# Convolution taps all on VectorE, and two of the small sums made by ScalarE and an adding DMA, in a convolution and hard-swish layer on one Trainium2 core

## The chip, the cores and the metric

The kernel runs on one core of a Trainium2 chip. The metric is device time in microseconds (us) of one launch. TensorE (PE) multiplies matrices, VectorE (DVE), ScalarE (ACT) and GpSimd (POOL) work on tiles, and SyncE (SP) issues transfers. Each of them takes its instructions in the order in which they were written down. Transfers (DMAs) are issued by SP, by POOL and by ACT and are carried by 16 DMA engines that all issuers share. A DMA issued by POOL can add what it carries to what already stands at its destination; this kernel uses that in place of additions on an engine.

## The reference

```python
# x: (8, 4096, 192), weight: (8, 7), w_in: (192, 2048), w_out: (2048, 192), all float32 in use
w = softmax(weight, axis=-1)                    # 8 heads x 7 taps
x_pad = concat([zeros(8, 6, 192), x], axis=1)   # causal
conv[b, s, head] = sum_k w[head, k] * x_pad[b, s + k, head]   # 24 channels per head
h = conv.reshape(32768, 192) @ w_in             # first layer
g = h * clip(h + 3, 0, 6) / 6
out = g @ w_out                                 # second layer
```

The two weight matrices arrive as 64-bit floats and are rounded in the kernel; x arrives transposed, channels ahead of time.

## The kernel before

The 32,768 tokens are worked in 32 blocks of 1,024, each as two groups of 512 that lie on the two halves of the partitions. Block 0 is computed in a plain way while the weights are prepared. Blocks 1 to 31 run the loop `for i in range(1, NB)` at the end of the kernel: `first_layer(i, jobs)` and then `second_layer(i, between)`.

**Convolution.** `y` (128 x 1536) holds the convolution of the next block. It takes seven steps, made by `conv_jobs`: ACT writes `x * c0` (L1030), and six taps add `x shifted by k, times c_k` to it. A tap is one DVE instruction (L1032). One of the six goes another way, `tap_by_dma` (L1019): POOL multiplies x into `S3` (L1021) and then issues a DMA that adds `S3` to `y` (L1025). When `y` is finished it is split into three parts, HIGH (ACT, L476), LOW (DVE, `split_low`, L1055) and MIX (DVE, `split_mix`, L479), from which the first layer gets float32 precision out of fast matmuls. Three pairs of POOL DMAs copy the parts to the other half of the partitions (`y_other`, L266 and L267).

**First layer.** 16 units, `n` = 0 to 15; units 0 to 7 read `y_own`, 8 to 15 `y_other`. A unit is 12 matmuls (`begin`), a multiplication in PSUM by ACT (L523), 6 more matmuls (`end`), then `relu` on ACT (L302) and `gate` on DVE (L306), which writes `g`. Four pairs of PSUM banks go round, so `begin(n + 4)` needs the banks that `gate(n)` gives back. In the last unit the multiplication is shared: ACT takes the lower bank (L526), DVE the upper (L527). `jobs[n]` is what is recorded behind unit n, `jobs[-1]` ahead of unit 0: here the convolution's taps, and `left`, the two `finish` steps that end the block before. On POOL, small sums of `g` into `shared` follow units 1, 3, 5 and 7, and then sums of `A22`, differences `S3` and DMAs that make `S1` (L561).

**Second layer.** `g` is read as a 2 x 2 matrix of quarters A11, A21, A12, A22, and the product is made in Strassen's way with seven products, some of them split a second time into seven small ones. For the first level the sums are S1 = A21 + A22, S2 = S1 - A11, S3 = A11 - A21, S4 = A12 - S2; S4 is written over S3, pair of chunks by pair of chunks, by `negative`: ACT writes -S2 (L696) and a POOL DMA adds A12 to it (L697). For the second level `small_sums(to, x, which, ...)` (L573) makes four sums of the quarters of x; `A12`'s go to `sums2` (a part of the tile `z2`), `S1`'s to `s5`, which is A22's place in `g`, and `A22`'s to `sums4`. The fourth sum is the second quarter of x less the second sum.

The order is written out by hand. PE's matmuls stand in four streams of 80 ticks each that run side by side in four column groups, and `do(t, fn)` records other engines' work at tick `t - 0.5`. All is sorted by tick and recorded in that order, so each engine's own order follows from the ticks. PE has one queue: when a matmul of one stream waits, the matmuls recorded behind it, of all four streams, wait as well. What the change touches stands at these ticks: product 7 with S3 up to tick 44; the small product (2, 3), which reads the fourth sum of A12, at ticks 60 to 64; product 3, which reads the four pairs of S4, from ticks 64, 68, 72 and 76; the small product (5, 3), which reads the fourth sum of S1, at ticks 72 to 76. `between` has the work for the next blocks: the taps left over at tick 24, `begin_conv` (a load of x by SP, into the one buffer that the taps have read) at 30, the split of y at 37, 62 and 63, its copies to the other half at 70, and the first step of the next convolution at 74.

Of the kernel before, what the change touches and what calls it, by code (L numbers as in the profile page):

```python
# [8 lines left out]
ALU = mybir.AluOpType  # L9
# [16 lines left out]
def kernel(  # L26
# [8 lines left out]
    nc = tc.nc  # L35
# [3 lines left out]
    H, KC = weight.shape  # L39
# [3 lines left out]
    N = 512  # L43
# [3 lines left out]
    K3 = D // D2  # L47
# [29 lines left out]
    def load_x(i, dma=nc.sync):  # L77
        x = xs.tile([P, K3, PAD + N], F32, name="x")
        head, lower, upper = x_source(i)
        if head:  # L80
            nc.vector.memset(x[0:D2, :, 0:PAD], 0.0)
        dma.dma_start(out=x[0:D2, :, head:], in_=lower)
        dma.dma_start(out=x[D2:P, :, :], in_=upper)
        return x
# [3 lines left out]
    for base, dma in ((0, nc.scalar), (D2, nc.sync)):  # L88
        dma.dma_start(
            out=w_sb[base : base + D2],  # L90
            in_=weight.unsqueeze(1).to_broadcast([H, GJ, KC]),
# [126 lines left out]
    for n in range(AHEAD):  # L218
# [8 lines left out]
        out=e_sb[:], in0=w_sb[:], in1=mx[:].to_broadcast([P, KC]), op=ALU.subtract  # L227
# [3 lines left out]
    c_sb = cst.tile([P, KC], F32, name="c_sb")  # L231
# [5 lines left out]
    y = ys.tile([P, K3, N], F32, name="y")  # L237
# [36 lines left out]
    A11, A21, A12, A22 = (g4[:, :, j] for j in range(4))  # L274
    S2, S1, S4 = A11, A21, A12
# [181 lines left out]
    def add(out, x, y, op=ALU.add):  # L457
        nc.vector.tensor_tensor(out=out, in0=x, in1=y, op=op)
# [33 lines left out]
    def swap_parts(dma=nc.sync, parts=range(3)):  # L492
        if parts[0] == HIGH:
            y_other[0] = pools[1].tile([P, 3, K3, N], F32, name="y_other", tag="other")
        for n in parts:
            swap(y_other[0][:, n], y_own[n], dma)
# [73 lines left out]
    def four_parts(x):  # L570
        return [x[:, c::2, t] for t in halves for c in range(2)]
# [30 lines left out]
    def second_layer(i, between):  # L602
# [3 lines left out]
        z = pools[1].tile([P, NP + 1, N], F32, name="z2", tag="other")  # L606
        sums2, p1 = z[:, 0:NP], z[0:DH, NP]
        ends = [psum[:, 2 * free_slots[0] + k] for k in range(2)] if last else [b, b]
        s5 = A22
# [21 lines left out]
        def do(t, fn, *args, **kw):  # L631
            streams[3].append((t - 0.5, lambda: fn(*args, **kw)))  # L632
# [58 lines left out]
        def fold(p, m136):  # L691
            add(p[second, hi], p[second, hi], p[second, lo])
            add(p[second, lo], m136, p[second, lo])

        def negative(pair):
            nc.scalar.mul(S3[:, pair], S2[:, pair], -1.0)  # L696
            nc.gpsimd.dma_start(out=S3[:, pair], in_=A12[:, pair], accum_op=ALU.add)  # L697

        def after(j, fn, *args, **kw):
            do(clock[j], fn, *args, **kw)  # L700
# [36 lines left out]
        left = [list(every) for _ in halves]  # L737
# [72 lines left out]
        do(32, fold_with, p1)  # L810
        do(33, g_sums, nc.vector, (2,), every[4:], 4)
        do(35, copy, out=b[m], in_=p1)
        do(36, small_sums, s5, S1, (1, 2, 3, 4), nc.vector)
        do(37, small_sums, sums2, A12, (4,), nc.vector)
        do(38, fold_with, p4, 2)
        for n, t in zip(range(0, NP, 2), (34, 39, 42, 45)):
            do(t, negative, slice(n, n + 2))
# [85 lines left out]
    with tc.manual_schedule():  # L903
# [4 lines left out]
            out=c_sb[:], in0=e_sb[:], in1=sm[:].to_broadcast([P, KC]), op=ALU.mult  # L908
# [15 lines left out]
        for _ in range(3):  # L924

            nc.tensor.matmul(
                out=psum[:, b], lhsT=zeros[:, 0:P], rhs=zeros[:], start=True, stop=True
# [58 lines left out]
        n = 3  # L986
# [29 lines left out]
        late = ctx.enter_context(tc.tile_pool(name="late", bufs=1, reuse_waits="tile"))  # L1016
        w_in_parts = [late.tile([P, NP, K3, P], F32, name=f"w_in{n}") for n in range(3)]

        def tap_by_dma(x, k):  # L1019
            to = S3[:, 0:K3]  # L1020
            nc.gpsimd.tensor_scalar(  # L1021
                out=to, in0=x[:, :, k : k + N], scalar1=c_sb[:, k : k + 1], scalar2=None,
                op0=ALU.mult,
            )
            nc.gpsimd.dma_start(out=y[:], in_=to, accum_op=ALU.add)  # L1025

        def conv_jobs(i):
            x = x_tiles.pop(i)
            conv_x[:] = [x]
            jobs = [lambda: nc.scalar.mul(y[:], x[:, :, 0:N], c_sb[:, 0:1])]  # L1030
            for k in range(1, KC):
                jobs.append(lambda k=k: nc.vector.scalar_tensor_tensor(  # L1032
                    out=y[:], in0=x[:, :, k : k + N], scalar=c_sb[:, k : k + 1], in1=y[:],
                    op0=ALU.mult, op1=ALU.add,
                ))
            return jobs
# [24 lines left out]
        def prepare():  # L1061
            for n in range(0, NP, 4):
                r = slice(n, n + 4)
                w_parts(*[w[:, r] for w in w_in_parts], w_in[:, r])
            for job in conv_jobs(1):
                job()
            first_in.close()
            later = ctx.enter_context(tc.tile_pool(name="later", bufs=1, reuse_waits="tile"))
            pools.append(later)
            pools.append(ctx.enter_context(tc.tile_pool(name="oth", bufs=1, reuse_waits="tile")))  # L1070
            x_tiles[2] = load_x(2, nc.gpsimd)
            split_y()

        conv, conv_x = [], []

        def begin_block_two():
            w_sums(((T1, B12, B11), (T2, B22, T1), (T4, B21, T2)))
            small_weights([(w_s[:, n], w) for n, w in enumerate((B11, T1, B21, T4))])
            conv.extend(conv_jobs(2))
            for job in conv[:2]:  # L1080
                job()
# [5 lines left out]
        S3 = last.tile([P, NP, N], F32, name="s3")[:]  # L1087
        left = []
        taps = conv[2:]
        for i in range(1, NB):  # L1090
            jobs = {3 + 2 * n: [tap] for n, tap in enumerate(taps[:5]) if n}
            k = KC - len(taps)
            jobs[-1] = [lambda: tap_by_dma(conv_x[0], k)] * bool(taps) + left
            first_layer(i, jobs)
            now = taps[5:]

            def begin_conv():
                x_tiles[i + 2] = load_x(i + 2)
                conv[:] = conv_jobs(i + 2)

            between = [(24, tap) for tap in now]
            conv = []
            if i + 1 < NB:
                between += [(37, split_high), (62, split_low), (63, split_mix)]
                between += [
                    (t, lambda n=n: swap_parts(nc.gpsimd, (n,)))
                    for n, t in ((HIGH, 70), (LOW, 70), (MIX, 70))
                ]
            if i + 2 < NB:
                between += [(30, begin_conv), (74, lambda: conv[0]())]  # L1110
            left = second_layer(i, between)
            taps = conv[1:]

# [32 lines left out]
```

## Time and profile before

| what | us |
|---|---|
| median of 3 runs (2389.35 to 2394.75) | 2394.53 |
| the profiled execution, its device time | 2391.43 |
| its span, first to last instruction | 2389.6 |
| PE busy in the span | 2271.1 |
| DVE busy | 2019.1 |
| ACT busy | 1694.2 |
| POOL busy | 1364.8 |
| PE idle ahead of first-layer matmuls (L511) | 84.5 |
| PE idle ahead of second-layer matmuls (L635) on `g` | 21.9 |

The profile is of one execution; its times are 0.1% under the median of the runs. A group in the profile is a source line, an engine, an operation and its operands, with the number of its instructions, their busy time in us, the mean of one in ns, and the idle time of the engine just before them with what ended it. The trace behind it has the start and the end of each instruction. Lines of helpers such as L584 (`small_sums`) or L635 (`matmul`) gather the work of several callers, so groups are told apart by operands and shapes: the sums of `S1` on DVE are `g<-g 128x1024`, those of `A12` and `A22` `z<-...`.

### The profile page before, as it was taken

How to read it: one execution, taken by the hardware profiler on the slowest of the kernel's cores; microseconds unless marked ns; L12 is line 12 of the kernel's file. 1: busy time of each engine (PE TensorE's matmuls, PEld its weight loads, DVE VectorE, ACT ScalarE, POOL GpSimd, SP SyncE). 2: the span in 40 equal slices, each digit the busy share in tenths (PEclk: the TensorE clock that was granted, in tenths of full speed). 3: DMA queues.
4: the chain of work that ended last, by engine and by line, in shares of the span. 5: the costliest groups of instructions: out<-in, count | busy, mean ns of one | idle time of the engine just before them, and what ended most of it. 6: DMA issues, size and time to landing. Idle time of an engine off the chain costs nothing.

```text
span 2389.6 us, 55082 instructions
## 1 busy us (share of the span) xinstructions
PE 2271.1 (95%) x22984; PEld 1479.5 (62%) x22984; DVE 2019.1 (84%) x1891; ACT 1694.2 (71%) x2329; POOL 1364.8 (57%) x1155
## 2 busy tenths in 40 slices
PE   9999999999999999999999999999999999999998
PEld 5456666666665566665666656666556666566665
DVE  8788888888788988889888898888898888988876
ACT  7567776677776777766777667677667776677765
POOL 2556665556655566555666455665556655566644
PEclk9999999999999999999999999999999999999999
DMA  5356668666676656685666766667755677566665
GB/s 146 81 100 122 116 116 151 116 113 116 117 142 131 109 114 118 134 151 96 118 121 124 147 117 113 114 119 142 139 101 112 116 137 147 101 118 119 123 122 85
DMA packets 308521, 288.00 MB, mean 121 GB/s; under 512 B 211472, under 2 KB 216592, under 8 KB 308272
## 3 DMA queue, kind: packets, MB, share of 16 engines
q0 software_dynamic: 86560, 225.55, 49.9%
q1 hardware_dynamic: 220472, 58.67, 13.5%
q8 instruction: 180, 2.95, 0.5%
q14 instruction: 69, 0.57, 0.1%
q10 hardware_dynamic: 1240, 0.27, 0.1%
HBM read 31.72 MB, written 25.17 MB: 24 GB/s over the span
## 4 chain that ended last, share of the span: by engine, by line
PE 51%; DMA 16%; DVE 12%; POOL 10%; issue 7%; ACT 3%; SPq 1%; DVEq 0%; POOLq 0%; ACTq 0%
PE psum L635 41%; DMA y<-s 11%; PE psum L511 7%; DVE g L306 6%; DVE y L1032 5%; POOL s L1021 4%; DMA out_dram<-shared 3%; PE psum L296 2%; PE psum L341 2%; POOL y_other L267 2%; POOL y_other L266 1%; ACT psum L632 1%; POOL shared L584 1%; DMA g<-g 1%; ACT g L302 1%
## 5 line engine op out<-in xcount | busy, mean ns | idle before, releaser
L635 PE MATMUL psum<-g,w_out 128*32 128x512 f32 (+1 forms) x5968 | 904.3, 520 | 21.9 <-DMA g<-g 12.6
L306 DVE SCALAR_TENSOR_TENSOR g<-g,psum 128x1024 f32<-128x1024 f32 (+1 forms) x528 | 613.3, 1182 | 189.5 <-ACT g L302 189.4
L635 PE MATMUL psum<-s,w_out 128*32 128x512 f32 (+1 forms) x3024 | 676.0, 587 | 1.2 <-DMA s<-g 1.2
L511 PE MATMUL psum<-y_other,w_in 64*128 64x512 f32 x4464 | 552.2, 393 | 84.5 <-DVE psum L527 51.4
L302 ACT ACTIVATE g<-psum,half 128x1024 f32<-128x1024 f32 (+1 forms) x528 | 567.4, 1087 | 50.9 <-PE psum L511 50.0
L511 PEld LDWEIGHTS psum<-y_other,w_in 64*128 64x128 f32 x4464 | 422.7, 185 | 203.0 <-DVE psum L527 64.0
L523 ACT ACTIVATE psum<-psum 128x1024 f32<-128x1024 f32 x465 | 469.0, 1009 | 102.0 <-PE psum L511 100.0
L635 PEld LDWEIGHTS psum<-g,w_out 128*32 128x32 f32 x5968 | 355.3, 113 | 297.1 <-issue 126.5
L511 PE MATMUL psum<-y_own,w_in 64*128 64x512 f32 x4464 | 521.9, 388 | 0.0
L511 PEld LDWEIGHTS psum<-y_own,w_in 64*128 64x128 f32 x4464 | 424.2, 184 | 105.4 <-issue 26.0
L697 POOL DMA_DIRECT2D s<-g x124 | 148.4, 1197 | 431.8 <-ACT s L696 405.9
L1032 DVE SCALAR_TENSOR_TENSOR y<-x,c_sb,y 128x1536 f32<-128x1536 f32 x156 | 351.7, 2255 | 46.4 <-DMA y<-s 44.2
L584 POOL TENSOR_TENSOR shared<-g 128x256 f32<-128x256 f32 x248 | 230.3, 929 | 103.0 <-DVE g L306 103.0
L635 PE MATMUL psum<-g,w_s 128*32 128x256 f32 x1488 | 283.5, 380 | 0.0
L635 PEld LDWEIGHTS psum<-s,w_out 128*32 128x32 f32 x3024 | 187.8, 110 | 85.8 <-issue 24.9
L635 PE MATMUL psum<-z,w_out 128*32 128x256 f32 x992 | 235.1, 380 | 2.4
L635 PE MATMUL psum<-z,w_s 128*32 128x256 f32 x992 | 237.0, 383 | 0.3 <-DVE z L584 0.2
L584 POOL TENSOR_TENSOR z<-g 128x1024 f32<-128x1024 f32 x62 | 205.3, 3311 | 0.0
L266 POOL DMA_DIRECT2D y_other<-y_own x90 | 48.8, 542 | 265.3 <-issue 246.6
L561 POOL DMA_DIRECT2D g<-g x124 | 150.0, 1224 | 86.4 <-DVE s L414 61.9
L414 POOL TENSOR_TENSOR s<-g 128x1024 f32<-128x1024 f32 x62 | 163.6, 2639 | 0.0
L414 DVE TENSOR_TENSOR g<-g 128x2048 f32<-128x2048 f32 x62 | 142.0, 2290 | 19.9 <-issue 18.9
(115 smaller groups left out, 2973.3 us busy)
## 6 DMA issues: line engine op xcount, KB each, us to landing
y_other<-y_own POOLq DMA_DIRECT2D x180, 384.0 KB, 8.1
g<-g POOLq DMA_DIRECT2D x124, 512.0 KB, 5.5
s<-g POOLq DMA_DIRECT2D x124, 512.0 KB, 6.6
out_dram<-shared SPq DMA_DIRECT2D x378, 64.0 KB, 5.5
y<-s POOLq DMA_DIRECT2D x30, 768.0 KB, 11.0
x<-in_x_dram SPq DMA_DIRECT2D x53, 388.5 KB, 5.7
stage<-in_moe_w_in_dram SPq DMA_DIRECT2D x16, 192.0 KB, 5.1
stage<-in_moe_w_out_dram SPq DMA_DIRECT2D x8, 384.0 KB, 5.5
```

Of the source, the lines that this page charges most:

```text
L266: dma.dma_start(out=to[D2:P], in_=part[0:D2])
L302: nc.scalar.activation(r6, h, ACT.Relu, bias=half[:], scale=1.0 / 6.0)
L306: nc.vector.scalar_tensor_tensor(out=g_, in0=g_, scalar=1.0, in1=h, op0=ALU.min, op1=ALU.mult)
L414: engine.tensor_tensor(out=o[:, r], in0=a[:, r], in1=b[:, r], op=op)
L511: nc.tensor.matmul(out=psum[:, 2 * slots[n] + k], lhsT=r32(w_in_parts[part][r, c, s]), rhs=r32(y_other[0][r, part, s] if group else y_own[ ...
L523: nc.scalar.mul(both(n), both(n), 4097.0)
L561: nc.gpsimd.dma_start(out=S1[:, pair], in_=A22[:, pair], accum_op=ALU.add)
L584: engine.tensor_tensor(out=o, in0=p, in1=q, op=op)
L635: nc.tensor.matmul(out=out, lhsT=w, rhs=x, start=start, stop=True, tile_position=(0, j * QS), skip_group_check=True,)
L697: nc.gpsimd.dma_start(out=S3[:, pair], in_=A12[:, pair], accum_op=ALU.add)
L1021: nc.gpsimd.tensor_scalar(out=to, in0=x[:, :, k : k + N], scalar1=c_sb[:, k : k + 1], scalar2=None, op0=ALU.mult,)
L1032: jobs.append(lambda k=k: nc.vector.scalar_tensor_tensor(out=y[:], in0=x[:, :, k : k + N], scalar=c_sb[:, k : k + 1], in1=y[:], op0=ALU.mu ...
```

## The change

- `tap_by_dma` is gone. All six taps of a block are DVE instructions. Four are recorded in the first layer, ahead of unit 0 and behind units 1, 3 and 5; before, they stood behind units 5, 7, 9 and 11, and the tap by DMA ahead of unit 0. Two are recorded at tick 24 of the second layer, before it was one.
- `left` is recorded ahead of the tap that stands ahead of unit 0.
- The fourth small sum of A12 and that of S1 leave DVE. A new `last_sum` lets ACT write the negated second sum into the place of the fourth, and a POOL DMA adds the quarter of A12 or S1. They are recorded at ticks 29 and 50; before, DVE made them behind the other sums at 37 and 36.
- `split_low` moves from tick 62 to 56, `begin_conv` from 30 to 27.

```diff
+        def difference(out, x, y):
+            nc.scalar.mul(out, y, -1.0)
+            nc.gpsimd.dma_start(out=out, in_=x, accum_op=ALU.add)
+
         def negative(pair):
-            nc.scalar.mul(S3[:, pair], S2[:, pair], -1.0)
-            nc.gpsimd.dma_start(out=S3[:, pair], in_=A12[:, pair], accum_op=ALU.add)
+            difference(S3[:, pair], A12[:, pair], S2[:, pair])
+
+        def last_sum(to, x):
+            z = four_parts(to)
+            difference(z[3], four_parts(x)[1], z[1])
...
-        do(36, small_sums, s5, S1, (1, 2, 3, 4), nc.vector)
-        do(37, small_sums, sums2, A12, (4,), nc.vector)
+        do(29, last_sum, sums2, A12)
+        do(36, small_sums, s5, S1, (1, 2, 3), nc.vector)
+        do(50, last_sum, s5, S1)
...
-        def tap_by_dma(x, k):
-            to = S3[:, 0:K3]
-            nc.gpsimd.tensor_scalar(
-                out=to, in0=x[:, :, k : k + N], scalar1=c_sb[:, k : k + 1], scalar2=None,
-                op0=ALU.mult,
-            )
-            nc.gpsimd.dma_start(out=y[:], in_=to, accum_op=ALU.add)
-
...
-            jobs = {3 + 2 * n: [tap] for n, tap in enumerate(taps[:5]) if n}
-            k = KC - len(taps)
-            jobs[-1] = [lambda: tap_by_dma(conv_x[0], k)] * bool(taps) + left
+            jobs = {2 * n - 1: [tap] for n, tap in enumerate(taps[:4])}
+            jobs[-1] = left + jobs.get(-1, [])
             first_layer(i, jobs)
-            now = taps[5:]
+            now = taps[4:]
...
-                between += [(37, split_high), (62, split_low), (63, split_mix)]
+                between += [(37, split_high), (56, split_low), (63, split_mix)]
...
-                between += [(30, begin_conv), (74, lambda: conv[0]())]
+                between += [(27, begin_conv), (74, lambda: conv[0]())]
```

The fourth parts are 128 partitions x 4 chunks x 256 floats, so a row of the new transfers is 1 KB long; a row of those of `negative` is 2 KB, two rows to a partition. Each of them carries 512 KB.

More of the change, by code (lines that the diff above doesn't have):

```diff
@@ L1017 @@
         w_in_parts = [late.tile([P, NP, K3, P], F32, name=f"w_in{n}") for n in range(3)]
-        def tap_by_dma(x, k):
-            to = S3[:, 0:K3]
-            nc.gpsimd.tensor_scalar(
-                out=to, in0=x[:, :, k : k + N], scalar1=c_sb[:, k : k + 1], scalar2=None,
-                op0=ALU.mult,
-            )
-            nc.gpsimd.dma_start(out=y[:], in_=to, accum_op=ALU.add)
         def conv_jobs(i):
             x = x_tiles.pop(i)
-            conv_x[:] = [x]
             jobs = [lambda: nc.scalar.mul(y[:], x[:, :, 0:N], c_sb[:, 0:1])]
@@ L1072, in prepare @@
             split_y()
-        conv, conv_x = [], []
+        conv = []
         def begin_block_two():
```

## The prediction

> **What bounds the kernel now.** First the page: busy time by engine, then the groups.
>
> ```profile
> PE 2271.1 (95%) x22984; PEld 1479.5 (62%) x22984; DVE 2019.1 (84%) x1891; ACT 1694.2 (71%) x2329; POOL 1364.8 (57%) x1155
> ...
> L1032 DVE SCALAR_TENSOR_TENSOR y<-x,c_sb,y 128x1536 f32<-128x1536 f32 x156 | 351.7, 2255 | 46.4 <-DMA y<-s 44.2
> L584 DVE TENSOR_TENSOR g<-g 128x1024 f32<-128x1024 f32 x124 | 146.1, 1220 | 1.1
> ...
> L696 ACT ACTIVATE s<-g 128x1024 f32<-128x1024 f32 x124 | 130.6, 1053 | 1.1
> ...
> L1021 POOL TENSOR_SCALAR s<-x,c_sb 128x1536 f32<-128x1536 f32 x30 | 125.9, 4196 | 0.6
> ```
>
> PE is the bound, with 118 us idle. The waits tell where:
>
> ```profile
> DVE y L1032 <- DMA y<-s: 44.2, 28, 3.2
> PE psum L511 <- DVE psum L527: 51.4, 23, 2.2
> PE psum L511 <- DVE g L306: 33.0, 31, 2.7
> ```
>
> The last two are PE waiting, late in the first layer, for a DVE that is behind. One such end, DVE and then PE in the timeline (start, us, engine, line):
>
> ```profile
> 1235.96 4.05 DVE L1032 SCALAR_TENSOR_TENSOR y<-x,c_sb,y 128x1536 f32<-128x1536 f32 x1
> 1239.94 1.21 DVE L306 SCALAR_TENSOR_TENSOR g<-g,psum 128x1024 f32<-128x1024 f32 x1
> 1241.07 0.69 DVE L527 TENSOR_SCALAR psum<-psum 128x512 f32<-128x512 f32 x1
> ...
> 1241.81 0.96 PE L511 MATMUL psum<-y_other,w_in 64*128 64x512 f32 x5 [2.21 <-DVE psum L527]
> ```
>
> The tap behind unit 11 took 4.05 us, beside a POOL operation on `g`, against a median of 1.82 for all taps; L527 came 3 us after ACT's half of the same job (1238.05), and PE stood for 2.21.
>
> From the timeline I took the starts of both layers in every block. Over blocks 1 to 30 a first layer with the gap behind it is 37.27 us, a second layer 36.35, together 73.62. Undisturbed they are 34.15 (block 31, which has no taps) and 35.06 (12 blocks). 1.7 us of many second layers is the clock, here at the start of one (busy time in a stretch: us; PE, PEld, DVE, ACT, POOL; clock, DMA share, GB/s):
>
> ```profile
> 2308.50:2342.65 34.15, 32.98 (x293) 26.83 (x289) 21.07 (x21) 32.01 (x33) 24.18 (x26) 1.00 0.53 104
> 285.29:288.63 3.34, 3.34 (x24) 1.52 (x28) 3.34 (x3) 0.99 (x1) 2.90 (x2) 0.50 0.09 15
> ```
>
> The first row is block 31's first layer, the second has a granted clock of 0.50. There are 17 such stretches of 3.41 us, mostly behind a PE stall of 2 us or more; each costs 1.7 us, 16 of them in blocks 1 to 30, 0.9 a block.
>
> Last, the second layer of the block that starts it at 1242.93: DVE, ACT, SP's load of x, and the transfers that turn S3 into S4:
>
> ```profile
> 1253.73 1.81 DVE L1032 SCALAR_TENSOR_TENSOR y<-x,c_sb,y 128x1536 f32<-128x1536 f32 x1
> 1255.46 2.29 DVE L414 TENSOR_TENSOR g<-g 128x2048 f32<-128x2048 f32 x1
> ...
> 1267.09 0.58 ACT L818 COPY shared<-psum 96x512 f32<-96x512 f32 x1
> ...
> 1255.69 0.54 SPq L82 DMA_DIRECT2D x<-in_x_dram  x1
> ...
> 1260.14 1.19 POOL L697 DMA_DIRECT2D s<-g  x1 [9.41 <-ACT s L696]
> 1263.48 1.19 POOL L697 DMA_DIRECT2D s<-g  x1 [2.15 <-ACT s L696]
> 1264.95 1.20 POOL L697 DMA_DIRECT2D s<-g  x1 [0.28 <-ACT s L696]
> 1267.36 1.20 POOL L697 DMA_DIRECT2D s<-g  x1 [1.21 <-DVE shared L458]
> ```
>
> By the completion times these four took 5.3, 5.0, 6.7 and 8.0 us, so they landed at 1265.4, 1268.5, 1271.7 and 1275.4. The last two are issued faster than they land: the landings of the last two pairs are 3.2 and 3.7 us apart, over all blocks 3.1 on the mean, and 256 packets of 2 KB, 192 ns each by the trace, on 16 engines are 3.1 us as well. POOL's transfers are carried one after the other, and four of them fill that queue until 1275.4. PE needs them at ticks 64, 68, 72 and 76; a tick is 35.06 / 80 = 0.438 us, so at 1271.0, 1272.7, 1274.5 and 1276.2. The fourth has under 1 us left.
>
> **The first layer gains.** Without the DMA into `y` the DVE wait (44.2 us in all) goes, and the taps leave the second half. I walk DVE from a first layer's start with block 31's pace: `relu(n)` ends at 5.3 + 2.04 n, PE needs the banks of `gate(n)` at 7.5 + 2.04 n, `left` ends at 3.6, a tap is 1.8, a gate 1.15. Tap to 5.4, gates 0 and 1 to 8.4, tap to 10.15, gates 2 and 3 end at 11.3 and 12.45, tap to 14.2, gates 4 and 5 to 16.5, tap to 18.25, gate 6 to 19.4. The tightest, gates 2, 4 and 6 (11.3, 15.3, 19.4), stand against 11.6, 15.7 and 19.75: no stall. With taps of 2.25 (the mean) up to 1.2 us of stall. From unit 9 DVE is on time, and L527 follows its matmuls. I take 34.3 (34.15 to 35.3) for 37.27: -3.0 a block. PE's short-clock stretches at the layer's end go with the stalls.
>
> POOL loses 4.2 + 0.9 us a block, off the path once that DVE wait is gone.
>
> **DVE in the second layer** gets one tap (+1.8) and loses two sums (-2 x 1.22). S2's first half starts behind the second tap; DVE enters 0.5 us earlier (in block 31 its sums end at 10.3 after PE's start, here 10.8), so that half comes 1.3 us later and ACT, which has slack of 1.0 there, loses some 0.2. `split_low` at 56 fills a DVE idle of 1.81 us; without that cover it would cost 1.7.
>
> **The two new transfers.** ACT's negation of A12's sum (1.05) fits in an ACT idle of 1.43 us ahead of 1257.16; its DMA is issued at about 1256.9. The load of x waits for the second tap and moves from 1255.69 to 1256.9, into the same time. S1's negation stands behind L818, so ACT makes it from 1267.7 to 1268.75; the copy behind it (L724, 1267.80) is 1.0 late, which its 1.1 us until tick 60 (1269.2) just covers; 0.2 us a block without. POOL issues the DMA at 1268.8, behind the fourth of S4. The swaps of `y_other` queue behind that; their cover is some 10 us.
>
> With 5.0 us, the least of the four, S1's transfer would land at 1273.8, in time for tick 72 (1274.5). But it is the sixth in a queue. A price for 1 KB packets no row has: not below the 3.1 us of equal bytes, not above 6.1 (twice the packets at 192 ns). Adding packets take 192 ns at 2 KB and, from the transfer into `y`, 493 at 6 KB; the line through both gives 117 at 1 KB, x 512 / 16 = 3.7 us, which I take, being near the 2 KB row. Then: x (384 packets of 143 ns, 3.4 us) and A12's transfer share the engines from 1258.6 (the first S4 transfer's 5.3 less its own 3.1, less the end, is a lead of 1.7) and end at 1265.7; four of 3.1 end at 1278.1; S1's ends at 1281.8. PE, and behind the small product (5, 3) all four streams, stands from 1274.5: 7.3 us a block. Bounds: if x and A12's transfer delay nothing and the last takes 3.1, it lands at 1278.5, 4.0 us late; with 6.1 for both new ones 12.1. PE's two idle times of 2.8 and 2.9 us on a DMA into `g` (blocks 14 and 31) were each followed by half clock, so a longer one will be: 1.7.
>
> The Trainium skill, DMA: Bandwidth & Descriptors, section "Why small descriptors are slow (HBM only)", says that transfers within SBUF do not pay for small rows. By it each new transfer would be 3.1 us, the stall 6.1 and the time 36 us less, an estimate from that page; the trace has 0.094 ns a byte at 2 KB against 0.080 at 6 KB, so some price there is. No run here shows 1 KB.
>
> **Sum.** 34.3 + 35.06 + 7.3 + 1.7 = 78.4 against 73.62: +4.7 a block, x 30 = +142. Block 31 has no x to load; its last S4 transfer lands 36.6 into the layer, S1's some 4 later, which I put at +3. 2391.4 + 145 = 2536 on the profiled execution's own time, 0.1% under the median of the runs, which is less than any step here.
>
> **Rivals.**
> - Faster: transfers overlap after all and S1's lands within its 5 to 5.5 us. For it: the issue at 1268.8 leaves 5.7. Against: 8.0 us of the fourth. Block: 34.3 + 35.1 = 69.4, -4.2 x 30: 2265. It turns at a stall and clock loss of 4.2 us together.
> - Least queueing: 4.0 us of stall, x loaded in the gap. With the clock loss 75.1, so 2435; without it 73.4, so 2384.
> - The first layer gains nothing, because ACT with 32.0 of 34.15 us busy is its limit or the early taps stall it: 37.3, so 2626. Against: block 31 ran in 34.15 with the same ACT.
> - Small rows at 6.1 us each: a stall of 12.1, 2680.
> - The change does not do what it says: DVE loses two sums and gains a tap, so it is hardly relieved (-0.6 a block); what it gets is a place for the taps. That is in the sum already.
>
> **How the numbers follow.** The forecast (2536, its own range 2470 to 2600) 0.55; least queueing with the clock loss 0.16, without it 0.05; transfers overlap 0.10; no gain 0.07; dear rows 0.07. Least queueing without the clock loss is at the edge of no change, so 0.04 of it counts as faster and 0.01 as the same, with 0.02 of the case above it. Faster 0.14, same 0.03, slower 0.83 (0.3% is what a measurement here can tell). The range 2395 to 2640 leaves out the overlap, the case without clock loss and most of the dear rows.
>
> **What would show it.** In the changed profile: L635 waiting on a DMA into `g` once a block, 4 to 12 us long; L527 no longer a releaser of PE; first layers near 34.3 us; half clock behind each long wait. A stall under 3 us a block, or a DMA that overtakes the fourth of S4, makes the prediction wrong.

## The result, and the profile after

The change makes the kernel slower: 2542.11 us (median of 4 runs, 2541.43 to 2547.1) against 2391.94 us, a ratio of 1.0637 with a 95% interval of 1.0608 to 1.0667. The prediction was 2536 us.

The page of the changed kernel, busy time by engine and the two groups that answer to those shown before (L1031 is now the line of the taps):

```profile
PE 2323.8 (92%) x22984; PEld 1482.3 (58%) x22984; DVE 1935.0 (76%) x1859; ACT 1758.3 (69%) x2391; POOL 1294.2 (51%) x1157
...
L635 PE MATMUL psum<-g,w_out 128*32 128x512 f32 (+1 forms) x5968 | 955.9, 518 | 202.4 <-DMA g<-g 166.1
...
L1031 DVE SCALAR_TENSOR_TENSOR y<-x,c_sb,y 128x1536 f32<-128x1536 f32 x186 | 360.7, 1939 | 2.6 <-ACT y L1029 1.3
```

DVE makes 30 taps more and 62 sums less and is busy for 84 us less: a tap is 1.94 us on the mean where it was 2.26, and taps wait for no transfer (2.6 us of idle time, before 46.4). PE's idle time ahead of second-layer matmuls on `g` went from 21.9 to 202.4 us, most of it on a DMA into `g`. The waits of PE, longest first in total (us, times, longest):

```profile
PE psum L635 <- DMA g<-g: 166.1, 32, 6.3
...
PE psum L635 <- DVE g L306: 36.3, 31, 1.2
```

Of the two waits of before, the one on L527 (51.4 us) is gone from the list, and the one in the first layer on L306 (33.0) is down to 0.2 us (weight loads still wait there, as shown further down). The end of one first layer shows why, in the timeline of ACT and then DVE:

```profile
1228.17 0.58 ACT L526 ACTIVATE psum<-psum 128x512 f32<-128x512 f32 x1 [0.34 <-PE psum L511]
```

```profile
1226.85 1.22 DVE L306 SCALAR_TENSOR_TENSOR g<-g,psum 128x1024 f32<-128x1024 f32 x1 [0.82 <-ACT g L302]
1228.21 0.70 DVE L527 TENSOR_SCALAR psum<-psum 128x512 f32<-128x512 f32 x1
1230.07 2.35 DVE L306 SCALAR_TENSOR_TENSOR g<-g,psum 128x1024 f32<-128x1024 f32 x2 [1.16 <-ACT g L302]
```

L527 now starts 0.04 us behind ACT's half (L526), before it was 3 us. What is lost in exchange is in the second layer of the same block, which starts at 1231.35. POOL's transfers there in the timeline, with the two new ones first and last:

```profile
1246.10 1.30 POOL L697 DMA_DIRECT2D z<-g  x1 [7.49 <-ACT shared L734]
1248.87 1.19 POOL L697 DMA_DIRECT2D s<-g  x1 [1.46 <-ACT s L696]
1252.20 1.19 POOL L697 DMA_DIRECT2D s<-g  x1 [2.15 <-ACT s L696]
1253.68 1.20 POOL L697 DMA_DIRECT2D s<-g  x1 [0.28 <-ACT s L696]
1256.09 1.20 POOL L697 DMA_DIRECT2D s<-g  x1 [1.21 <-ACT s L696]
1257.65 1.30 POOL L697 DMA_DIRECT2D g<-g  x1 [0.36 <-ACT g L696]
```

The page's list of transfers has their size and the median from issue to landing in us (S1's stand among `g<-g`):

```profile
g<-g POOLq DMA_DIRECT2D x155, 512.0 KB, 6.3
...
s<-g POOLq DMA_DIRECT2D x124, 512.0 KB, 8.4
...
z<-g POOLq DMA_DIRECT2D x31, 512.0 KB, 8.8
```

Those of S4 took 6.6 before. The one of S1 at 1257.65 took 11.7 us from issue to landing and landed at 1269.35, and this is PE in its timeline:

```profile
1269.41 0.64 PE L635 MATMUL psum<-g,w_out 128*32 128x256 f32 x1 [5.41 <-DMA g<-g]
```

Tick 72 would have been at 1231.35 + 31.55 = 1262.9, so the block lost 6.5 us there (the idle time shown is shorter because matmuls of product 3 still ran until 1264.0). The same stretch by windows (us; busy PE, PEld, DVE, ACT, POOL; granted clock, DMA share, GB/s): the first layer, the second layer up to the wait, the rest of it, and the half clock:

```profile
1196.71:1231.35 34.64, 33.41 (x289) 26.68 (x289) 27.86 (x24) 32.03 (x33) 25.47 (x21) 1.00 0.30 54
1231.35:1263.80 32.45, 32.36 (x402) 17.41 (x402) 30.66 (x30) 22.51 (x41) 12.19 (x10) 1.00 0.87 157
1263.80:1275.30 11.50, 6.09 (x35) 2.02 (x32) 1.48 (x3) 0.37 (x1) 3.13 (x6) 0.70 1.08 210
1267.31:1274.13 6.82, 4.72 (x28) 1.91 (x29) 0.43 (x1) 0.37 (x1) 0.09 (x1) 0.50 1.02 232
```

The DMA engines are nearly full over the second layer (share 0.87, then 1.08; packets that overlap on an engine count twice). The half clock begins within the wait and lasts 4.7 us beyond it, which costs 2.4 us more.

### The profile page after: what moved, and what is told of

The parts are those of the page before. It is cut to its first block, busy times and chain, and to the rows that moved or that the text cites. A ratio compares the mean times of both kernels' runs of the same rounds, so it can differ in the third digit from the quotient of the medians.

```text
span 2539.6 us, 55266 instructions
## 1 busy us (share of the span) xinstructions
PE 2323.8 (92%) x22984; PEld 1482.3 (58%) x22984; DVE 1935.0 (76%) x1859; ACT 1758.3 (69%) x2391; POOL 1294.2 (51%) x1157
## 4 chain that ended last, share of the span: by engine, by line
PE 62%; DMA 14%; DVE 14%; ACT 7%; issue 1%; POOL 1%; SPq 0%; ACTq 0%; DVEq 0%; POOLq 0%
PE psum L635 37%; PE psum L511 22%; DMA g<-g 14%; DVE g L306 8%; DVE y L1031 6%; ACT g L302 3%; PE psum L296 2%; PE psum L341 2%; ACT psum L523 1%; ACT psum L632 1%; ACT z L734 0%; ACT shared L734 0%; POOL shared L584 0%; DMA x<-in_x_dram 0%; POOL s L414 0%
## 5 line engine op out<-in xcount | busy, mean ns | idle before, releaser
L635 PE MATMUL psum<-g,w_out 128*32 128x512 f32 (+1 forms) x5968 | 955.9, 518 | 202.4 <-DMA g<-g 166.1
L306 DVE SCALAR_TENSOR_TENSOR g<-g,psum 128x1024 f32<-128x1024 f32 (+1 forms) x528 | 615.5, 1183 | 190.0 <-ACT g L302 189.6
L635 PE MATMUL psum<-s,w_out 128*32 128x512 f32 (+1 forms) x3024 | 746.4, 663 | 0.8 <-DMA s<-g 0.8
L635 PEld LDWEIGHTS psum<-g,w_out 128*32 128x32 f32 x5968 | 372.6, 113 | 569.0 <-issue 202.0
L584 POOL TENSOR_TENSOR shared<-g 128x256 f32<-128x256 f32 x248 | 320.4, 1292 | 496.8 <-DVE g L306 480.0
L511 PE MATMUL psum<-y_other,w_in 64*128 64x512 f32 x4464 | 528.3, 389 | 1.6
L511 PEld LDWEIGHTS psum<-y_own,w_in 64*128 64x128 f32 x4464 | 413.5, 184 | 117.8 <-issue 26.4
L511 PEld LDWEIGHTS psum<-y_other,w_in 64*128 64x128 f32 x4464 | 413.6, 184 | 106.3 <-DVE g L306 21.6
L1031 DVE SCALAR_TENSOR_TENSOR y<-x,c_sb,y 128x1536 f32<-128x1536 f32 x186 | 360.7, 1939 | 2.6 <-ACT y L1029 1.3
L458 DVE TENSOR_TENSOR shared<-psum,shared 32x256 f32<-32x256 f32 (+2 forms) x159 | 83.2, 523 | 303.0 <-ACT shared L734 262.3
L734 ACT COPY shared<-psum 32x256 f32<-32x256 f32 x62 | 22.6, 365 | 300.4 <-PE psum L635 300.4
L584 POOL TENSOR_TENSOR z<-g 128x1024 f32<-128x1024 f32 x62 | 163.8, 2642 | 0.0
```

What stands on the lines that cost most here:

```text
L306: nc.vector.scalar_tensor_tensor(out=g_, in0=g_, scalar=1.0, in1=h, op0=ALU.min, op1=ALU.mult)
L511: nc.tensor.matmul(out=psum[:, 2 * slots[n] + k], lhsT=r32(w_in_parts[part][r, c, s]), rhs=r32(y_other[0][r, part, s] if group else y_own[ ...
L584: engine.tensor_tensor(out=o, in0=p, in1=q, op=op)
L635: nc.tensor.matmul(out=out, lhsT=w, rhs=x, start=start, stop=True, tile_position=(0, j * QS), skip_group_check=True,)
L1031: jobs.append(lambda k=k: nc.vector.scalar_tensor_tensor(out=y[:], in0=x[:, :, k : k + N], scalar=c_sb[:, k : k + 1], in1=y[:], op0=ALU.mu ...
```

## The experiments

Eight more kernels were run. The table has the means of blocks 1 to 30 from each trace: a first layer with the gap behind it, a second layer, and when the last of POOL's transfers of S4 and of the fourth sums landed, counted from the second layer's start.

| kernel | device us | first layer | second layer | last landing |
|---|---|---|---|---|
| before | 2391.9 | 37.27 | 36.35 | 33.4, S4 |
| after | 2542.1 | 34.67 | 43.75 | 37.8, S1 |
| E1: S1's sum on DVE | 2296.1 | 34.66 | 35.77 | 33.8, S4 |
| E2: A12's sum on DVE | 2491.2 | 34.65 | 42.09 | 36.4, S1 |
| E3: both on DVE | 2294.3 | 34.65 | 35.80 | 32.5, S4 |
| E4: the kernel before with both by DMA | 2571.6 | 36.20 | 43.25 | 37.7, S1 |
| E5: S1's ahead of S4's fourth pair | 2413.2 | 34.71 | 39.46 | 37.5, S4 |
| E6: moved ticks back | 2532.4 | 34.65 | 43.52 | 37.6, S1 |
| E7: E3 with late taps | 2371.7 | 36.40 | 36.60 | 33.5, S4 |
| E8: E3 with `split_low` at 62 | 2272.5 | 34.65 | 35.08 | 32.6, S4 |

**E1, S1's fourth sum back on DVE.**

```diff
-        do(36, small_sums, s5, S1, (1, 2, 3), nc.vector)
-        do(50, last_sum, s5, S1)
+        do(36, small_sums, s5, S1, (1, 2, 3, 4), nc.vector)
```

> S1's fourth sum goes back to DVE, A12's stays with the adding DMA. Queue theory (PE waits because S1's transfer is the sixth in POOL's one-after-another queue and lands 37.9 us into the second layer, needed at 31.55): with five transfers the last is the fourth pair of S4, which lands as in the changed kernel at 33.8 us against a need at 33.3, so a wait of 0.5 us or less, no half clock, a block of 34.67 + 35.06 + 0.6 = 70.3 instead of 78.4 us; about 2293 us, faster than the kernel before. Rival, that the loss comes from the taps (DVE too full in the second layer with two taps): DVE gets 1.2 us more here, and the time would stay near 2540 or grow.

2296.1 us (one run). Without this one transfer the whole loss is gone, and the kernel is faster than before. S4's fourth pair lands 0.5 us late, as expected, and the waits on it are small:

```profile
PE psum L635 <- DMA s<-g: 15.4, 24, 1.6
```

**E2, A12's fourth sum back on DVE.**

```diff
-        do(29, last_sum, sums2, A12)
...
         do(50, last_sum, s5, S1)
+        do(37, small_sums, sums2, A12, (4,), nc.vector)
```

> A12's fourth sum goes back to DVE, S1's stays with the adding DMA. Queue theory: S1's transfer is then the fifth, and nothing but the load of x is ahead of the four of S4; it lands near 36.0 us, 4.5 late, and half clock costs 1.7 to 2.5 behind it: a block of 76 to 76.7 us, about 2480 us. If the two new transfers were equally at fault, half of the loss of 150 us would go: 2467. If S1's transfer were late for ACT's negation alone (issued at 26.4, 5 us from issue to landing), A12's would not matter: 2540.

2491.2 us (one run). PE's wait on it is shorter, 124.4 us in all:

```profile
PE psum L635 <- DMA g<-g: 124.4, 32, 4.7
```

S1's transfer lands at 36.4 in place of 37.8. So A12's transfer, which nobody waits for, delays S1's by 1.4 us through the queue, and 26.4 (its issue) + 5 is not what sets the landing. The two are not equally at fault either: E1 took off 246 us, E2 51.

**E3, both back on DVE; the taps as the change has them.**

```diff
-        do(29, last_sum, sums2, A12)
-        do(36, small_sums, s5, S1, (1, 2, 3), nc.vector)
-        do(50, last_sum, s5, S1)
+        do(36, small_sums, s5, S1, (1, 2, 3, 4), nc.vector)
+        do(37, small_sums, sums2, A12, (4,), nc.vector)
```

> Both fourth sums go back to DVE; the taps stay where the change put them and tap_by_dma stays away. Queue theory: four transfers as before, no wait on them; first layer with its gap 34.67 us, second layer 35.06 us plus 0.1, clock at full: 69.8 us a block, 2542 - 30 x 8.6 - 6 = 2278 us, 4.8% faster than before. Rival, that two taps at tick 24 delay S2 and S4 so far that PE waits: second layer over 36 us, time over 2310.

2294.31 us (4 runs), 0.9582 of before (0.9549 to 0.9614; before had a median of 2396.23 beside it). The part of the change that concerns the taps is a gain of 4.2%. The expectation missed 16 us: the second layer is 35.80 us, not 35.1. The waits of this kernel say where:

```profile
PEld psum L635 <- DVE shared L458: 29.8, 29, 1.6
PE psum L635 <- DVE shared L458: 15.8, 29, 1.1
```

PE waits once a block for a DVE addition (E8 follows this up).

**E4, the kernel before with only the two sums changed.** Its diff is that of the change in `second_layer`, without the lines on taps, `split_low` and `begin_conv`.

> The kernel before with only the two fourth sums moved to ACT and the adding DMA; taps and tap_by_dma as before. Queue theory: first layers stay at 37.3 us, second layers go from 36.35 to about 43.5 (S1's transfer near 37.5 us, 6 late, and 2.5 us by half clock): 80.8 us a block, 2391 + 30 x 7.2 + 6 = 2613 us, more than the whole change. Rival, that the sums cost nothing by themselves and only collide with the second tap: 2390 to 2420.

2571.6 us (one run): slower than the whole change, as the queue theory says, but 41 us better than it said. Second layers came as expected (43.25 for 43.5). First layers became 1.1 us shorter, because PE's long wait gave POOL time to be done with its copies to the other half: it issues the last of them 4.5 us ahead of the first layer's start, in the kernel before 2.1 behind it, and the transfer into `y` 0.9 us behind that start, before 7.2 (means). The taps hardly wait for it any more (44.2 us before):

```profile
DVE y L1040 <- DMA y<-s: 1.9, 1, 1.9
```

**E5, S1's transfer ahead of S4's fourth pair.**

```diff
-        do(50, last_sum, s5, S1)
+        do(44.6, last_sum, s5, S1)
```

> The changed kernel with S1's ScalarE negation and adding DMA recorded at tick 44.6, ahead of the fourth pair of S4, not at 50. Queue theory: the sum of the six transfers stays and the last of them, now S4's fourth pair, lands near 37.9 us into the second layer but is needed at 33.3 only; S1's lands near 34.6 (2.5 to 3 us late), S4's fourth 1 to 1.5 more: 4.5 us of waiting in two pieces in place of 6.3, a block near 76.5 us, about 2485 us. Rival, that only the late issue of S1's transfer (26.4) matters: the issue 1.5 us earlier takes 1.5 us off at most where nothing else waits, 2497 us and one wait; or, if the queue did not matter, S1's transfer would land 5.3 us after its issue, at 30.2, and no wait were left: near 2300.

2413.2 us (one run). S1's lands at 34.0, S4's fourth pair at 37.5, and the second layer is 4.4 us over its undisturbed 35.06: the transfers' sum, not S1's own latency, sets what is lost, in two waits:

```profile
PE psum L635 <- DMA s<-g: 48.1, 30, 2.8
PE psum L635 <- DMA g<-g: 47.7, 31, 2.5
```

It is 72 us better than expected because half clock hardly comes: in 3 of blocks 1 to 30, against all 30 in the changed kernel, where most stretches are twice as long (24 us in the whole trace against 213). Two waits of 0.7 to 2.8 us with work between them did not bring it on in most blocks.

**E6, two of the moved ticks back.**

```diff
-                between += [(37, split_high), (56, split_low), (63, split_mix)]
+                between += [(37, split_high), (62, split_low), (63, split_mix)]
...
-                between += [(27, begin_conv), (74, lambda: conv[0]())]
+                between += [(30, begin_conv), (74, lambda: conv[0]())]
```

> The changed kernel with the split's low part back at tick 62 and the load of x back at 30. Theory: SP has nothing between the two ticks, and VectorE waits for nobody there while PE stands for S1's transfer: no change, 2542 us within 0.5%. Rival, that the earlier load of x is what collides with the transfers: 1 to 2 us a block less, 2490 to 2510.

2532.4 us (one run), 0.4% under the changed kernel's median: within what was expected, and too little for one run to tell from nothing.

**E7, E3 with the first layer's taps where they stood before.**

```diff
-            jobs = {2 * n - 1: [tap] for n, tap in enumerate(taps[:4])}
+            jobs = {2 * n + 5: [tap] for n, tap in enumerate(taps[:4])}
```

> All sums on VectorE and no tap by DMA, as in the 2294 us version, but the four taps of the first layer stand behind units 5, 7, 9 and 11, their place in the kernel before. Theory (VectorE is late at the layer's end because of where the taps stand, beside POOL's sums of whole quarters): the first layer goes back to 36.5 to 37.3 us, L527 is late again, half clock follows some of these waits; 2294 + 30 x 2.2 to 3.3 = 2360 to 2393 us. Rival (it was the wait for the transfer into y that made VectorE late): first layer 34.7 to 35.3, 2294 to 2315 us.

2371.7 us (one run). First layers go from 34.65 to 36.40 us, and PE waits for the late L527 again:

```profile
PE psum L511 <- DVE psum L527: 64.8, 29, 2.2
```

So of the 2.6 us by which a first layer got shorter, the place of the taps is worth 1.75. The other 0.87 is what E7 keeps over the kernel before, and the tap by DMA is the likely cause, though E7 differs from that kernel in more: PE's wait on L306 within the first layer (33.0 us before) is not among E7's. E4 agrees: it keeps the tap by DMA, but the taps do not wait for it, L306 is down to 1.7 us, and its first layers take 36.20.

**E8, E3 with the low part of the split back at tick 62.**

```diff
-                between += [(37, split_high), (56, split_low), (63, split_mix)]
+                between += [(37, split_high), (62, split_low), (63, split_mix)]
```

> The 2294 us version (all sums on VectorE, taps early) with the split's low part back at tick 62. In that version PE waits 0.5 to 0.7 us a block at 28.7 us into the second layer, when product 3 has to overwrite a bank that VectorE's addition at tick 60.2 still reads; the low part (1.7 us) stands ahead of that addition. Theory: behind it, the wait goes: second layer 35.1 in place of 35.8, 2294 - 30 x 0.65 = 2275 us. Rival, that VectorE is late there for the second tap and the extra sums: no change, 2294.

2272.45 us (5 runs, 2271.89 to 2273.95), 0.9502 of before (0.9487 to 0.9516; before had a median of 2391.82 beside it), and the best of all. The wait on L458 is gone and second layers are at 35.08. PE's share on its page:

```profile
PE 2221.7 (98%) x22984; PEld 1452.9 (64%) x22984; DVE 2002.5 (88%) x1921; ACT 1693.8 (75%) x2329; POOL 1214.4 (53%) x1095
```

## Why the prediction was right, point by point

The time is right, and the mechanism is the one that was forecast. A block was forecast at 78.4 us and is 78.42. That it comes so close is luck: its terms are off by 0.4 to 1.0 us and cancel.

- **First layer**, 34.3 forecast, 34.67 measured. The walk of DVE through taps and gates held for the first two taps. The third and the fourth took 2.2 us on the mean and not 1.8, and the pair of gates behind the fourth starts late:

```profile
1213.53 2.25 DVE L1031 SCALAR_TENSOR_TENSOR y<-x,c_sb,y 128x1536 f32<-128x1536 f32 x1
1215.70 2.34 DVE L306 SCALAR_TENSOR_TENSOR g<-g,psum 128x1024 f32<-128x1024 f32 x2
```

This layer starts at 1196.71, so gate 6, the first of the pair, ends at 20.2 and not at 19.4, past the 19.75 at which PE needs it. What waits is not a matmul but the weight loads:

```profile
PEld psum L511 <- DVE g L306: 22.3, 61, 0.6
```

That is the 0.5 us by which these layers are longer than block 31's; the forecast named such a stall for longer taps and took it at nearly nothing. The gap of 1.17 us ahead of each second layer (the 36.3 us on L306) was in the forecast's 34.15. The prediction put DVE's lateness down to the wait for the transfer and to the taps' place together; E7 puts 1.75 us on the place, and 0.87 on the rest.
- **The sixth transfer** was the right mechanism. E1 shows that without it the loss is gone, E2 and E5 that it is late by the queue ahead of it. Its size was 1 us too large: landing forecast at 38.9 (1281.8 in that block's clock), measured 37.8, so a wait of 6.3 us in place of 7.3. The term that was off is the four transfers of S4. They were priced at 3.1 us each, the spacing of before; with the queue never empty they follow each other in 2.5 to 2.8 us, 1.8 us less for the four. Two smaller errors take some of that back: A12's transfer lands 0.4 us later than forecast, and S1's lands 4.0 us behind the fourth of S4, not 3.7. The load of x is the other part of the queue: block 30, which has none, has A12's landing at 19.7 in place of 23.2 and S1's at 36.4.
- **The price of 1 KB rows**, taken as 117 ns a packet, is 111 ns on the mean and 102 in the middle: by the mean 3.6 us a transfer against 3.0 for the same bytes in 2 KB rows (187 ns, 185 in the middle). That is 19% more by the means, 10% by the middle values. The landings point to the lower figure: in E5, where S1's transfer is the fifth, it lands 2.9 us behind the one ahead of it, and the sixth, with 2 KB rows, 3.5 us behind that. So the last place is slow with either kind of row; why was not tried. Here the trace departs from the Trainium skill, DMA: Bandwidth & Descriptors, section "Why small descriptors are slow (HBM only)", by which transfers within SBUF do not pay for small rows; these adding ones paid 10 to 19%.
- **Half clock** was taken at 1.7 us a block and is 2.4: in 29 of 30 blocks two stretches of 3.41 us follow each other, on the mean from 2.1 us ahead of the wait's end to 4.7 behind it. This term's error (+0.7), the first layer's (+0.4) and the wait's (-1.0) nearly cancel.
- **Block 31** lost 6.1 us to the kernel's end, not 3.
- **`split_low` at 56** was costed at nothing, for a DVE idle of 1.8 us. That holds in the changed kernel, where PE waits anyway (E6 shows no gain from moving it back that one run can tell). Where DVE has the two sums as well, the cover is gone: 0.7 us a block (E3 against E8), less than the 1.7 named.
- Of the rivals, overlapping transfers are excluded by E2 and E5, a first layer without gain and dear rows by the measured parts. "Least queueing" (4.0 us) lies further off than the forecast.

## What to carry to other kernels

Work that is moved from a busy engine to a DMA joins a queue: count all transfers of that queue between the data's readiness and its first reader, with every other load on the same DMA engines, before taking the latency of one alone. A transfer that nobody waits for still delays the next one. A change of two parts can hide a gain: here the taps were worth 4 to 5% and the transfers cost over 10%, and only running each part alone showed it.

## What the runs showed of the hardware

A wait of PE costs more than itself when half clock follows. One wait of 3.5 to 6.3 us of idle PE was followed by it in every block of the changed kernel and in blocks 2 to 30 of E2, in stretches of 3.41 or 6.83 us, so that PE ran at half until 2.9 to 6.0 us beyond the wait's end. A similar loss cut into two waits (E5) was mostly free of it, with a mean granted clock of 0.995 against 0.959 in the changed kernel and 0.968 in E2. The length of a wait alone does not decide: single waits of 2.2 us on L527 at the end of a first layer were followed by such a stretch in 12 of 23 cases in the kernel before, 19 of 29 in E7 and all 25 in E4.

The stretches follow a fixed grid. In each of the seven traces with six or more of them, all their starts lie within 0.03 us of a grid with a period of 3.413 us, laid through the starts of that trace. In E2 the price goes with the wait's place on this grid, and not with its length. Its waits are alike, 3.6 to 4.7 us. The 15 that began 0.6 to 1.0 us behind a grid line had two stretches each, the 14 that began 2.9 to 3.4 us behind one had one, and the one that began 1.45 us behind a line had none. No run moved a wait along the grid on purpose.
